# Attention scores of seven of eight pairs as three float32r products instead of one float32 product

## The chip, the cores and the metric

One core of a Trainium2 chip. The time is device microseconds of one execution, from the device's own measurement; the profile is of another execution of the same program. In the profile PE is TensorE (products), PEld its weight loads, DVE VectorE, ACT ScalarE, POOL GpSimd, SP SyncE, whose queue issues nearly all transfers. L56 is line 56 of the kernel before.

## The reference, cut to what matters

```python
scores = scale * np.matmul(q, k.transpose(0, 1, 3, 2))
h = np.maximum((psi_rel / psi_i)[..., None] @ w1 + b1, 0.0)
scores = scores + (h @ w2).transpose(2, 0, 1)[None, :, :, :]
attn = np.exp(scores - np.max(scores, axis=-1, keepdims=True))
attn = attn / (np.sum(attn, axis=-1, keepdims=True) + 1e-09)
x = np.matmul(attn, v)
```

q, k and v are float32 of 2 x 8 x 576 x 64 (batch, heads, sequence, head dimension). Two feed-forward networks follow on the 1152 rows of x: one with 2048 hidden columns and a rational activation, then four experts of 1024 with a gate. The change does not touch them.

## The kernel before, in words

The first 58 us make a position bias per head. Then comes the attention stage, to about 190 us, and the two networks fill the rest, TensorE nearly without a gap.

The attention stage works on eight **pairs** n = 0 to 7: two heads of one batch entry. The 64 dimensions of one head lie on partitions 0 to 63, those of the other on 64 to 127, so that each head's score product uses one half of TensorE's rows. A pair has nine **units** u. Unit u below eight is head u % 2 and block u // 2 of 128 of the 576 query rows; unit 8 is the last 64 rows of both heads, on the upper and the lower 64 output partitions. A call `scores(u)` for even u (lines 514 to 529) makes units u and u + 1: for each half of 288 key columns and each head one float32 product of 64 rows. VectorE then (line 527) adds the bias and takes the least, ScalarE's `exp` (line 536) makes the exponential and its sum, and VectorE's `weights` (line 543) transposes blocks of 32 for the product with v.

The order is written out by hand in one loop (lines 701 to 715), over the list of all units in order; only pair zero's last units stand among pair one's first. One step of the loop, called (n, u) here after its unit, issues: the scores of the unit two ahead, if that is even; what stands in the list `later`; `exp` of the next unit; `weights` of its own; and then `fill(n, u)` (lines 652 to 691). Every engine runs its instructions in the order in which they are issued. `fill` spreads the rest over the steps:

- values of the pair before, in (n, 1), (n, 3), (n, 5) and (n, 7) (line 576, into the tile ob); after the last of them three copies of o to SBUF on ScalarE (line 589), and, through `later` in (n, 8), `put` on GpSimd: one product with the reciprocal rows rs (line 594), two casts and two subtractions (lines 597 and 598).
- in (n, 5), for n from one to five, `prep(n + 2)`: ten transposes of raw q and k on TensorE into ob (line 181), and `load_qk` of the pair after that into the same raw tiles, six transfers. In (n, 6) four copies on ScalarE (`copied`, line 186) bring the transposed q (times 0.125) and k into the tiles qs and ks. Pair one is prepared in (0, 1), pair two in (1, 1).
- after (n, 8), `inverse`: reciprocal of the sums on VectorE and three copies on GpSimd (lines 551 and 554). In (n + 1, 6) `turn` transposes these on TensorE, and ScalarE copies them to rs (line 564).
- four early pieces of the first network's weights, one a pair from pair three on (lines 624 to 633, `EARLY` in line 697), through `later`: in (n, 4) ScalarE's narrowing (line 359), in (n, 5) to (n, 7) three steps on VectorE (lines 361, 363, 365), and in (n + 1, 0) the first part on ScalarE (line 369) and the second on GpSimd (line 375). They share one narrowed buffer: a piece's line 359 waits for the line 375 of the piece before.
- loads of v (line 163) in (n, 8), copies of v to the other partitions (line 167) in (n, 1), weight words in (2, 4), (3, 4), (5, 6) and (7, 3).

The score tiles of PSUM (tag s) have two buffers, which `turn` and the scores share.

## Time and profile before

| | us |
|---|---|
| median of 3 runs (779.59 to 781.68) | 781.19 |
| the profiled execution | 778.81 |
| its span in the trace | 777.0 |
| busy: PE, DVE, ACT, POOL | 758.7, 551.3, 428.9, 266.8 |

The span runs from the first to the last instruction; 1.8 us of the profiled execution lie outside of it. A busy time is a sum over the whole program, and PE's is 98% of the span, but it tells nothing of which engine is waited for within the attention stage. The granted clock of TensorE was at full speed throughout.

### The profile page before, as it was taken

Reading aid. Unit: us, or ns where it says so; the run is one execution under the profiler, and the core shown is the slowest. Engines: PE = TensorE matmul, PEld = TensorE weight load, DVE = VectorE, ACT = ScalarE, POOL = GpSimd, SP = SyncE. Lnnn points to the kernel's source line nnn. Section 1 sums busy time; section 2 is a strip of 40 time slices with the busy share of each in tenths; the row PEclk is TensorE's granted clock in tenths of the full one; section 3 lists DMA queues with packets and bytes.
Section 4 is the critical chain, followed back from the end, with each engine's and each line's share of the span. In section 5 each row is a group of like instructions: output and inputs, shape, how many; then the busy total and the mean of one; then the engine's idle time right before and its main releaser. Section 6 shows DMA issues by size and latency. Waiting matters only on the chain. (4 is left out here: it accounts for less than half of the span.)

```text
span 777.0 us, 15918 instructions
## 1 busy us (share of the span) xinstructions
PE 758.7 (98%) x6470; PEld 657.5 (85%) x6470; DVE 551.3 (71%) x873; ACT 428.9 (55%) x689; POOL 266.8 (34%) x278
## 2 busy tenths in 40 slices
PE   8998999999999999999999999999999999999998
PEld 5445766668899999999998989989989989988987
DVE  7998889996999999998954535567545645644731
ACT  6986667765988888787733525244314423413500
POOL 0000223442453655643300201236436534723710
PEclk9999999999999999999999999999999999999999
DMA  8899687551331331402123434332212202212201
GB/s 147 198 218 214 129 192 166 134 116 51 104 114 55 98 120 55 163 2 81 54 83 117 155 97 147 109 110 95 81 55 82 82 28 81 82 49 75 67 28 55
DMA packets 83946, 79.41 MB, mean 102 GB/s; under 512 B 38017, under 2 KB 62977, under 8 KB 83201
## 3 DMA queue, kind: packets, MB, share of 16 engines
q1 hardware_dynamic: 83440, 78.39, 37.3%
q8 instruction: 51, 0.84, 0.4%
q14 instruction: 23, 0.18, 0.1%
q10 hardware_dynamic: 432, 0.01, 0.0%
HBM read 59.20 MB, written 2.36 MB: 79 GB/s over the span
## 5 line engine op out<-in xcount | busy, mean ns | idle before, releaser
L56 PE MATMUL hp<-x,wi 128*128 128x384 f32 x888 | 159.7, 337 | 1.4 <-DVE u L776 1.1
L56 PEld LDWEIGHTS hp<-x,wi 128*128 128x128 f32 x888 | 154.0, 188 | 4.1 <-PE yp L56 1.5
L56 PE MATMUL op<-w,h 128*128 128x512 f32 (+1 forms) x600 | 133.1, 382 | 0.6 <-DVE acc L895 0.6
L56 PEld LDWEIGHTS op<-w,h 128*128 128x128 f32 x600 | 109.5, 188 | 22.4 <-DVE acc L895 0.8
L56 PE MATMUL yp<-g_hi,w 128*128 128x384 f32 x384 | 102.1, 336 | 0.3 <-ACT y L832 0.3
L895 DVE SCALAR_TENSOR_TENSOR acc<-op,pr_sb,acc 128x512 f32<-128x512 f32 (+1 forms) x28 | 20.4, 730 | 72.8 <-PE op L56 72.8
L56 PEld LDWEIGHTS yp<-g_hi,w 128*128 128x128 f32 x384 | 69.7, 188 | 1.2 <-ACT y L832 0.6
L536 ACT ACTIVATE pq<-pq,nm 128x576 f32<-128x576 f32 x72 | 55.4, 771 | 16.3 <-DVE nm L527 16.1
L56 PE MATMUL yp<-g_lo,w 128*128 128x384 f32 x192 | 64.2, 334 | 0.0
L373 POOL TENSOR_TENSOR w<-stage,w 128x256 fp32r<-128x256 f32 x64 | 49.1, 798 | 35.5 <-ACT w L369 35.5
L527 DVE CUSTOM_DVE_ANT_0 pq<-sc,ba 128x576 f32<-128x576 f32 x72 | 51.6, 749 | 13.3 <-PE sc L56 13.1
L417 ACT ACTIVATE wi<-stage 128x1024 fp32r<-128x1024 f32 x16 | 17.0, 1061 | 77.8 <-POOL stage L415 77.8
L56 PE MATMUL op<-w,h_hi 128*128 128x512 f32 x192 | 59.2, 389 | 0.0
L56 PE MATMUL sc<-ks,qs 64*128 64x288 f32 (+1 forms) x320 | 55.7, 429 | 2.7 <-DVE nm L527 1.9
L756 POOL TENSOR_TENSOR g_lo<-u,g_hi 128x768 fp32r<-128x768 f32 x24 | 45.1, 1880 | 35.8 <-ACT g_hi L755 33.8
L369 ACT ACTIVATE w<-stage 128x1024 fp32r<-128x1024 f32 x32 | 33.7, 1055 | 37.8 <-DMA stage<-in_moe_w_dram 37.7
L543 DVE STREAM_TRANSPOSE pt<-pq 128x576 f32<-128x576 f32 x72 | 52.1, 753 | 0.0
L576 PE MATMUL o<-pt,val 32*64 32x160 f32 (+1 forms) x2304 | 48.8, 293 | 2.3 <-issue 1.9
L232 PE MATMUL bps<-hid,wb 128*32 128x288 f32 x576 | 46.9, 410 | 3.2 <-DVE hid L221 2.3
L576 PEld LDWEIGHTS o<-pt,val 32*64 32x64 f32 x2304 | 39.2, 130 | 12.8 <-issue 5.9
L1038 ACT ACTIVATE h<-part_sums 128x384 fp32r<-128x384 f32 x48 | 25.1, 523 | 43.0 <-DVE part_sums L1058 34.4
L221 DVE TENSOR_SCALAR hid<-tab,cut 128x576 f32<-128x576 f32 x112 | 48.4, 522 | 0.0
(141 smaller groups left out, 1425.6 us busy)
## 6 DMA issues: line engine op xcount, KB each, us to landing
stage<-in_moe_w_dram SPq DMA_DIRECT2D x48, 512.0 KB, 3.6
ba<-ev SPq DMA_DIRECT2D x32, 288.0 KB, 5.4
words<-in_moe_w_in_dram SPq DMA_DIRECT2D x8, 1024.0 KB, 5.6
words<-in_moe_w_out_dram SPq DMA_DIRECT2D x8, 1024.0 KB, 5.0
stage<-in_moe_w_dram SPq DMA_DIRECT2D x64, 128.0 KB, 2.4
val<-val SPq DMA_DIRECT2D x21, 288.0 KB, 4.0
val<-in_v_dram SPq DMA_DIRECT2D x11, 288.0 KB, 4.1
out_dram<-acc SPq DMA_DIRECT2D x8, 256.0 KB, 2.0
```

The lines of the kernel that those rows point to most:

```text
L56: pe.matmul(o, lhsT=l, rhs=r, start=start, stop=stop)
L221: dve.tensor_scalar(tiles[par], win, at, 0.0, ALU.add, ALU.max)
L232: pe.matmul(sc[32 * par:32 * par + 32, hf, :288], lhsT=wb.rearrange("p r h -> p (r h)"), rhs=tiles[par][:, 288 * hf:288 * hf + 288], start ...
L369: act.activation(t[:, :, 0, :], self.raw, AF.Copy)
L373: pool.tensor_tensor(t[:, x[0], 1, x[1]], self.raw[:, x[0], x[1]], f32(t[:, x[0], 0, x[1]]), ALU.subtract)
L527: dve.tensor_tensor_reduce(out=self.row(u + e).rearrange("p (a j) -> p a j", a=2), in0=o[:, :, :288], in1=bs.rearrange("p (a j) -> p a j", ...
L536: act.activation(self.row(u), self.row(u), AF.Exp, bias=least.pop((self.n, u)), scale=-1.0, accum_out=self.sm[:, u:u + 1])
L543: dve.transpose(self.pt[:, 5 * e + k], self.row(u))
L576: pe.matmul(self.o[64 * e:64 * e + 64, a, c:c + 32 * m], lhsT=val[self.n % 2][r, NKB * e + b], rhs=self.pt[r, i:i + m, 32 * b:32 * b + 32] ...
L756: pool.tensor_tensor(lo, u, f32(hi), ALU.subtract)
L895: dve.scalar_tensor_tensor(out=a, in0=op, scalar=pr_sb[:, j, e:e + 1], in1=a, op0=ALU.mult, op1=ALU.add)
L1038: act.activation(t[:, 0], v, AF.Relu)
```

## The change

Pairs one to seven split q and k into a first part rounded to float32r and a second part, the rest, also in float32r. A score is then the sum of three products, accumulated in PSUM: first by first, first by second, second by first. Pair zero stays in float32. The four copies from ob now go back into the raw tiles; from there ScalarE makes the first parts and GpSimd subtracts to make the second, k in the next step through `later`, q in the step after that. The last 64 query rows of the two heads lie in a block matrix `both` of 128 x 128 with zeros off the blocks, so that unit 8 is three full products per half instead of two on quarters of the array. The raw tiles are free only after the split, so the load of k moves to (n, 8) and that of q to (n, 0). Two weight buffers change their pool to make room.

```diff
--- before.py
+++ after.py
@@ -147,10 +147,11 @@
 
     val = [rp.tile([P, 2 * NKB, D], F32, tag=f"v{i}", name="val") for i in range(2)]
 
-    def load_qk(n):
+    def load_qk(n, which=(0, 1)):
 
         p, b = divmod(n, 2)
-        for x, y in zip(raw(n), (q, k)):
+        for i in which:
+            x, y = raw(n)[i], (q, k)[i]
             h = y[b, 2 * p:2 * p + 2]
             for e in range(2):
                 sp.dma_start(x[:, 0:4, e], h[e, 0:512].rearrange("(t p) d -> p t d", p=P))
@@ -185,13 +186,11 @@
             w = 256 + 64 * a
             act.activation(x[:, 256 * a:256 * a + w], tp[:, a, 192:192 + w], AF.Copy, scale=scale)
 
-    def qs_tile(n):
-        q_of[n] = qk.tile([P, S], F32, tag="qs", name="qs")
-        return q_of[n]
-
-    def ks_tile(n):
-        k_of[n] = qk.tile([P, S], F32, tag="ks", name="ks")
-        return k_of[n]
+    def qk_tile(of, n, name):
+        of[n] = [qk.tile([P, S], F32R if n else F32, tag=name, name=name)]
+        if n:
+            of[n].append(lows.tile([P, 512 if name == "qs" else S], F32R, tag=name, name=name))
+        return of[n]
 
     def prep_first(x, to, scale):
         tp = ps.tile([P, 1024], F32, tag="s", name="tp_qk")
@@ -263,7 +262,7 @@
     load_qk(0)
     load_v(0, 4)
     BESIDE = {0: cut_near, 2: lambda: inverse_psi(psi), 5: cut_far}
-    BESIDE.update({6: lambda: prep_first(raw_q, qs_tile(0), 0.125), 7: lambda: (prep_first(raw_k, ks_tile(0), 1.0), load_qk(1), load_qk(2))})
+    BESIDE.update({6: lambda: prep_first(raw_q, qk_tile(q_of, 0, "qs")[0], 0.125), 7: lambda: (prep_first(raw_k, qk_tile(k_of, 0, "ks")[0], 1.0), load_qk(1), load_qk(2))})
     for r in range(4):
         dve.tensor_scalar(wb[:, r], w2c, pick[:, 3 - r:4 - r], None, ALU.mult)
     for m in range(AHEAD):
@@ -290,7 +289,7 @@
     pools = {}
 
     def wtile(tag, shape, dt, name, bufs=1):
-        return pools[tag in ("wi0", "words0", "words1", "narrow0")].tile(shape, dt, tag=tag, name=name, bufs=bufs)
+        return pools[tag in ("words0", "words1")].tile(shape, dt, tag=tag, name=name, bufs=bufs)
 
     class Weight:
 
@@ -352,7 +351,7 @@
             if not self.w.w64:
                 return
             if step == 0:
-                self.raw = wtile("narrow0" if self.early else f"narrow{turn('narrow', 2)}", self.shape, F32, "narrow")
+                self.raw = ap.tile(self.shape, F32, name="narrow", bufs=1) if self.early else wtile(f"narrow{turn('narrow', 2)}", self.shape, F32, "narrow")
             lo, hi = self.words[:, :, :, 0], self.words[:, :, :, 1]
             st, u = self.raw, self.raw.bitcast(U32)
             if step == 0:
@@ -477,6 +476,7 @@
 
 
     pools[True] = ctx.enter_context(tc.tile_pool(name="weights", bufs=2, reuse_waits="tile", side="right"))
+    lows = pool_of("lows")
     sp_, ap, pts = pool_of("scores"), pool_of("attn"), pool_of("pts", "right")
     po = phase.enter_context(tc.tile_pool(name="po", bufs=1, space=PSUM, reuse_waits="tile"))
 
@@ -488,6 +488,7 @@
         return x_t[cc][:, c]
 
 
+    both = [lows.tile([P, 2, P], F32R, name=f"both{i}", bufs=1) for i in range(2)]
     sums_z = ap.tile([P, P], F32, name="sums_z", bufs=1)
 
     ob = po.tile([P, 4, 512], F32, tag="o", name="o")
@@ -495,9 +496,28 @@
     def prep(n):
         for x, a in zip(raw(n), (0, 2)):
             turned(x, [ob[:, a + t // 2 - t // 4, 192 + P * (t % 2 + t // 4 * 2):min(512, 320 + P * (t % 2 + t // 4 * 2))] for t in range(5)], n < 3)
-        if 1 < n < NN - 1:
-            load_qk(n + 1)
-        soon.append(lambda: (copied(ks_tile(n), ob[:, 2:4], 1.0), copied(qs_tile(n), ob[:, 0:2], 0.125)))
+        if n == 2:
+            load_qk(3)
+        q32, k32 = (x.rearrange("p t e d -> p (t e d)")[:, :S] for x in raw(n))
+
+        def split(of, name, x):
+            t = qk_tile(of, n, name)
+            w = 512 if name == "qs" else S
+            hi, lo = t[0][:, :w], t[1]
+            act.activation(hi, x[:, :w], AF.Copy)
+            pool.tensor_tensor(lo, x[:, :w], f32(hi), ALU.subtract)
+            for e in range(2 * (name == "qs")):
+                r = slice(64 * e, 64 * e + 64)
+                hi, lo = (both[n % 2][r, part, r] for part in range(2))
+                act.activation(hi, x[r, w:S], AF.Copy)
+                pool.tensor_tensor(lo, x[r, w:S], f32(hi), ALU.subtract)
+
+        def whole():
+            copied(k32, ob[:, 2:4], 1.0)
+            copied(q32, ob[:, 0:2], 0.125)
+            later.append(lambda: (split(k_of, "ks", k32), later.append(lambda: split(q_of, "qs", q32))))
+
+        soon.append(whole)
 
     def keep_warm():
         for _ in range(4):
@@ -517,10 +537,15 @@
             self.pq[k] = sp_.tile([P, 2 * S], F32, tag="pq", name="pq", bufs=3)
             sc = [ps.tile([P, 2, 512], F32, tag="s", name="sc") for _ in range(2 - u // 8)]
             for hf in range(2):
-                for e in range(2):
-                    rows, cols = slice(64 * e, 64 * e + 64), slice(k * P, min(S, (k + 1) * P))
-                    out = sc[e][:, hf, :288] if u < 8 else sc[0][rows, hf, :288]
-                    mm(out, q_of[n][rows, cols], k_of[n][rows, 288 * hf:288 * hf + 288], True, True)
+                products = ((0, 0), (0, 1), (1, 0)) if n else ((0, 0),)
+                for i, (qpart, kpart) in enumerate(products):
+                    if n and u == 8:
+                        mm(sc[0][:, hf, :288], both[n % 2][:, qpart], k_of[n][kpart][:, 288 * hf:288 * hf + 288], i == 0, i == 2)
+                        continue
+                    for e in range(2):
+                        rows, cols = slice(64 * e, 64 * e + 64), slice(k * P, min(S, (k + 1) * P))
+                        out = sc[e][:, hf, :288] if u < 8 else sc[0][rows, hf, :288]
+                        mm(out, q_of[n][qpart][rows, cols], k_of[n][kpart][rows, 288 * hf:288 * hf + 288], i == 0, i + 1 == len(products))
             for e, o in enumerate(sc):
                 bs = bias[k, self.p // 2][:, self.p if u == 8 else 2 * (self.p % 2) + e]
                 nm = const.tile([P, 1], F32, tag="nm", name="nm", bufs=4)
@@ -672,6 +697,10 @@
             keep_warm()
         if u == 8 and 0 < n < NN - 1:
             load_v(n + 1)
+        if u == 8 and 0 < n < NN - 3:
+            load_qk(n + 3, (1,))
+        if u == 0 and 1 < n < NN - 2:
+            load_qk(n + 2, (0,))
         if (n, u) in COPY_V:
             copy_v(COPY_V[n, u])
         if u == (8 if n else 7):
@@ -703,8 +732,10 @@
             n, u = units[i + 2]
             if u % 2 == 0:
                 pair[n].scores(u)
-        if i == 2:
+        if i == 0:
             pool.memset(sums_z, 0.0)
+            for x in both:
+                pool.tensor_copy(x, sums_z.unsqueeze(1).to_broadcast([P, 2, P]))
         catch_up(later)
         if 0 <= i + 1 < len(units):
             n, u = units[i + 1]
```

## Rows read from the trace of the kernel before

**Rows 1.** Busy time in pair five: stretch, length; PE, PEld, DVE, ACT, POOL busy (count); clock; DMA.
```profile
134.06:149.13 15.07, 14.68 (x345) 10.22 (x344) 14.21 (x32) 11.01 (x30) 6.04 (x9) 1.00 0.60 151
```

**Rows 2.** Waits from 77 to 118 us: who waited for whom, us in all, times, longest.
```profile
DVE pq L527 <- PE sc L56: 6.0, 9, 1.2
```

**Rows 3.** Waits from 118 to 177 us, same columns.
```profile
ACT narrow L359 <- POOL w L375: 4.9, 3, 1.7
...
DVE pq L527 <- PE sc L56: 2.8, 7, 0.7
```

**Rows 4.** Timeline of ScalarE, rs of pairs four and six: start, us, what [idle before].
```profile
132.55 0.65 ACT L564 ACTIVATE rs<-rt 128x576 f32<-128x576 f32 x1 [1.10 <-PE rt L56]
...
161.75 0.65 ACT L564 ACTIVATE rs<-rt 128x576 f32<-128x576 f32 x1
```

**Rows 5.** Timeline of TensorE in pair five, and all scores: durations min/median/max.
```profile
139.11 1.24 PE L56 MATMUL sc<-ks,qs 64*128 64x288 f32 x8
...
140.28 1.64 PE L576 MATMUL o<-pt,val 32*64 32x160 f32 x80
...
L56 PEld LDWEIGHTS sc<-ks,qs x320: 129/186/243, 58.5 to 174.7; 64*128 64x128 f32 x128, 64*64 64x64 f32 x32
...
L56 PE MATMUL sc<-ks,qs x320: 402/403/507, 58.5 to 174.9; 64*128 64x288 f32 x128, 64*64 64x288 f32 x32
```

**Rows 6.** Timeline of TensorE, float32r products of 256 columns; the same by form: busy us, mean ns.
```profile
770.77 3.13 PE L56 MATMUL op<-w,h 128*128 128x256 f32 x24 [0.58 <-DVE acc L895]
...
L56 PE MATMUL op<-w,h 128*128 128x256 f32 x48 | 6.2, 285 | 0.6 <-DVE acc L895 0.6
```

**Rows 7.** Timeline of ScalarE in pair five.
```profile
136.27 0.93 ACT L589 ACTIVATE x<-o 128x512 f32<-128x512 f32 x3 [1.11 <-PE o L576]
...
138.00 0.61 ACT L369 ACTIVATE w<-narrow 128x512 fp32r<-128x512 f32 x1
...
143.71 0.68 ACT L359 ACTIVATE narrow<-words 128x512 f32<-128x512 f32 x1 [1.60 <-POOL w L375]
...
145.82 0.76 ACT L536 ACTIVATE pq<-pq,nm 128x576 f32<-128x576 f32 x1
...
147.62 0.65 ACT L564 ACTIVATE rs<-rt 128x576 f32<-128x576 f32 x1 [0.96 <-PE rt L56]
```

**Rows 8.** Timeline of GpSimd in pair five.
```profile
137.27 1.42 POOL L594 TENSOR_TENSOR x<-x,rs 128x576 f32<-128x576 f32 x1 [8.82 <-ACT x L589]
...
139.18 0.59 POOL L598 TENSOR_TENSOR x<-x,x 128x192 fp32r<-128x192 f32 x1
...
140.30 1.01 POOL L598 TENSOR_TENSOR x<-x,x 128x384 fp32r<-128x384 f32 x1
...
142.41 1.27 POOL L375 TENSOR_TENSOR w<-narrow,w 128x512 fp32r<-128x512 f32 x1
```

**Rows 9.** Loads of q, copies of o, transposes in pair two: SyncE, ScalarE, TensorE timelines; landing.
```profile
86.72 0.93 SPq L156 DMA_DIRECT2D raw_q<-in_q_dram  x2
...
DMA to landing us min/median/max: 2.4/3.4/7.5
...
90.58 0.93 ACT L589 ACTIVATE x<-o 128x512 f32<-128x512 f32 x3 [0.90 <-PE o L576]
...
97.25 0.86 PE L181 MATMUL o<-ident,raw_q 128*128 128x128 f32 x5
```

**Rows 10.** Timelines of ScalarE and TensorE around pair one's first scores.
```profile
65.53 0.70 ACT L186 ACTIVATE qs<-o 128x256 f32<-128x256 f32 x2
...
69.19 1.24 PE L56 MATMUL sc<-ks,qs 64*128 64x288 f32 x6 [0.46 <-DVE nm L527]
```

**Rows 11.** Line 363 and 365 in all: min/median/max ns; GpSimd beside the longest.
```profile
L363 DVE SCALAR_TENSOR_TENSOR narrow<-words,narrow x18: 685/1226/2761, 117.1 to 335.8; 128x1024 uint32<-128x1024 uint32 x14, 128x512 uint32<-128x512 uint32 x4
...
L365 DVE SCALAR_TENSOR_TENSOR narrow<-words,narrow x18: 686/1224/1268, 120.1 to 337.1; 128x1024 uint32<-128x1024 uint32 x14, 128x512 uint32<-128x512 uint32 x4
...
315.95 2.30 POOL L756 TENSOR_TENSOR g_lo<-u,g_hi 128x768 fp32r<-128x768 f32 x1
```

## The prediction

> **What bounds the kernel now.** The change lies in the attention stage, so I first split that stage by pair (the busy time of each engine in one pair's stretch, with its length). [Rows 1]: in pair five TensorE is busy for 14.68 of 15.07 us, VectorE for 14.21, ScalarE for 11.01, GpSimd for 6.04. Two engines are close together and the third not far; the totals do not say which one ends last, so I went to the waits. [Rows 2]: from 77 to 118 us VectorE waits nine times, 6.0 us in all, for scores from TensorE: there TensorE bounds. [Rows 3]: from 118 to 177 us it is only 2.8 us in seven waits, and ScalarE waits three times, 4.9 us, for GpSimd's second parts of an early weight before it may narrow the next piece into the same buffer (line 359 behind line 375). ScalarE works in order, so everything behind that wait is late too: three exponentials, then the reciprocal rows rs, then the two copies that empty the transposes. How much lateness is free there, the idle time just before rs shows: 1.10 us in pair four, 0.96 in pair five, none in pair six [rows 4, 7].
>
> **The products.** A call for an even u below eight is now eight records, 1.24 us from first start to last end; where nothing is waited for, the next group starts 1.17 us after it (139.11 to 140.28 [rows 5]). Eight records of 0.40 us and more fit into 1.24 us only if the two heads' run side by side, on the two halves of the rows: the last pair starts 0.84 us after the first, so a pair of records takes some 0.24 us, four of them 0.96, with 0.2 us around them. The new call has six pairs of single-pass products of 288 columns. float32r products on half the rows do not occur in this trace. On all rows they do: 24 of 256 columns take 3.13 us from first start to last end, and one record 0.285, so they start (3.13 - 0.285)/23 = 0.124 us apart [rows 6]; by columns that is 0.139 for 288. If the halves run together the call is 6 x 0.139 = 0.83 us, 0.13 less; 0.12 each (half of 0.24) would make it 0.24 less. If they don't, it is 12 x 0.139 = 1.67 us, 0.71 more. I take the first, since float32 on the same rows is nearest in form. For u = 8, of the same records now, it is six full products, 0.83, against four times 0.24: also 0.13 less. That is 0.65 us of TensorE per pair, 4.6 us over seven pairs, if every call were waited for.
>
> On that the Trainium skill (TensorE: Matmul & The Clock Gate, Part 3, What overlaps and what doesn't) speaks against the change: a weight load passes a running product only when their row groups differ. With its load of 128 columns at P/1.2 ns (LDWEIGHTS), 107 ns estimated, six steps would be 1.36 us (6 x (0.107 + 0.12)) instead of 0.83. The trace disagrees: each of the 256-column products above brought its own weights in the same rows, at 0.124 us a piece.
>
> **The splits.** ScalarE keeps its four copies, now into the raw tile, and per pair gets four more: k (576 columns), q (512, nearest row 0.61 us, line 369 [rows 7]) and two of 64 x 64. GpSimd gets the subtractions: 576 columns, 1.42 us as line 594; 512 columns, 1.27 us as line 375 in the same form; two of 64 columns. Line 598 took 0.59 for 192 and 1.01 for 384 [rows 8], that is 0.18 + 0.0022 per column, 0.32 for 64; between 0.18 and 0.59. In total 3.3 us of GpSimd and about 1.7 of ScalarE. By busy time both fit. What matters is the order. k's split goes out in the iteration of (n, 7), ahead of the copies of o, where GpSimd idles (8.82 us before line 594 [rows 8]): free. q's split goes out in (n, 8) **ahead of** the five operations of put, the three of inverse, and the early weight's line 375. So GpSimd's line 594, now starting as soon as the three copies of o end (137.20), first has to wait for ScalarE's first part of q (0.61), then 1.27 + 2 x 0.32: it starts 2.5 us later, and line 375 ends 2.5 us later. It starts as late as that in pairs four, five and six, where a next piece waits for it. ScalarE's line 359 then starts 2.5 us later, and so do the three exponentials behind it (the last at 145.82, 0.76 us [rows 7]) and rs. Free [rows 4, 7] are 1.10, 0.96 and 0: 3 x 2.5 - 2.06 = **5.4 us** later. After rs come TensorE's next scores (the second tile waits for rs), the copies of k and q, the values and the copies of o that begin the next round, so this lateness adds up over the three pairs, and in these rounds the shorter products save nothing. Bounds: 0 if GpSimd's work elsewhere gives way, and 7.5 if nothing is free.
>
> VectorE's transposes wait for the exponentials too. In (n, 8) the split of q is also ahead of the first exponentials of the next pair: 0.61 + 2 x 0.2 us. That is inside the 2.5 us in pairs four to six, and about 0.1 us in pairs two and three.
>
> **The loads.** k of pair n+3 moves to the end of pair n and q of pair n+2 to (n, 0); q now waits until the last subtraction has read the raw tile, and on SP the copies of val and the words of the early weights queue behind it, all used a pair later, at no cost. Pair two: the copies of o start at 90.58, 0.93 us; first part 0.61, subtractions 1.9, so the load is issued at about 94.1; two issues took 0.93 us, then the third lands 2.4 to 3.4 us (least and median) after its own, so q is there by 97.4 to 98.4. The transposes started at 97.25 [rows 9]. So pair two and three's transposes come 0.3 us later each (0 to 1.2) instead of 0.4 earlier by three shorter calls. In pairs four and five VectorE's own lateness covers it.
>
> **The start.** Pair one's copies end at 66.23 and its scores' last six records begin at 69.19 [rows 10]. In between now stand k's first part, an exponential, q's first part and 1.27 us of subtraction: 66.23 + 0.65 + 0.76 + 0.61 + 1.27 = 69.5. The third product waits 0.3 us for it (0 to 1).
>
> **Other edits.** The memset of sums_z and the two block tiles are filled while GpSimd has nothing to do before the first pair's weights; without that cover three copies of 0.3 us. One weight buffer and one narrowed buffer change pools; they are first written after the attention stage, whose tiles are free by then; without that, one wait of the first conversion, under 1 us.
>
> **Sum.** Gains: four calls from the middle of pair one to the first of pair two 0.52, the last call of pairs two and three and the first of the next 0.52, one in pair seven 0.13, together 1.2. Losses: 5.4 + 0.6 (loads) + 0.3 (start) + 0.1. Net +5.2 us. The profiled execution took 778.81 us (span 777.0), 2.4 us under the median of 781.19. So 778.8 becomes 784.0, and I say **786.4** for the median. A measurement of this kernel tells some 0.3%, 2.3 us, from no change.
>
> **Rivals.**
> 1. *The cover holds, faster.* If the early weight's subtraction is not late enough to matter (its wait is 1.6 us of 15 [rows 7], and GpSimd has 9 us free per pair [rows 1]), only products count: sixteen waits [rows 2, 3] of which each shrinks by 0.13 to 0.24, 2.1 to 3.8 us, less 0.3: 777.5 to 779.5. Against it: order, not load, decides. Chance 0.17.
> 2. *Between the two*: about half of the 5.4 us is lost. 779.5 to 783. Chance 0.09.
> 3. *The halves do not run together, much slower.* 28 calls of 0.71 more less 7 x 0.13 = +19 us, less what VectorE and the ScalarE chain need in the same time anyway: 793 to 800. For it: no float32r row on half the rows. Against it: float32 does it. Chance 0.13.
> 4. *Weight loads do not pass products of their own rows.* With the 0.19 us of a score's load [rows 5] in front of each step, six steps are 6 x (0.139 + 0.19) = 1.97 us, 1.0 more in 28 calls: 805 and over. Against it are [rows 6]. Chance 0.02. It is the rule of the Trainium skill weighed above.
> 5. *GpSimd gets in VectorE's way.* One operation of line 363 took 2.76 us where 1.23 is the median, beside a GpSimd subtraction that took 2.30 [rows 11]. k's subtraction will fall on line 365, of the same form, in pairs three to five: 3 x 1.5 = 4.6 us more if the later exponentials don't cover it, 787 to 791. Against it: eighteen of line 365 took at most 1.27 us [rows 11]. Chance 0.03. The Trainium skill (GPSIMD Engine Reference, Key points) has it that GpSimd shares its SBUF interfaces with VectorE, and that operations with two SBUF inputs collide; by that rule all three would pay, and the trace agrees in the one case only.
>
> The forecast, 783 to 790, has 0.58 (no wait free, 7.5 - 5.4 more, and the loads' 1.8 more, at its top; half of the 2.5 us less in one pair at its bottom), the five rivals 0.17, 0.09, 0.13, 0.02 and 0.03. The range 778.0 to 792.0 takes in all but the two much slower ones and the best of the first. Faster by over 0.3%: most of the first rival, 0.14. Within it: the rest of that and the second, 0.14. Slower: 0.72.
>
> **What would show it.** Right: records of 64-row products in pairs, six steps in about 0.8 us; ScalarE's three waits at line 359 near 4 us each; line 594 starting 2.5 us after the copies of o end; no idle before rs. Wrong: waits at line 359 as before, or score calls of 1.6 us and more.

## The result, and the profile after

The changed kernel takes **790.4 us** (median of 4 runs, 788.28 to 792.15), the kernel before 780.47 beside it (4 runs, 779.59 to 781.68): ratio 1.0125, 95% interval 1.0094 to 1.0156, 9.9 us slower. The forecast was 786.4, with a range from 778 to 792. The profiled execution took 789.86 us, its span 788.1, which is 11.1 more than before.

Where the 11.1 us arise is read from one operation that each call of the scores has once or twice, VectorE's step that adds the bias and takes the least for the exponential (line 527 before, line 552 now; I call it the exponent step). I took the start of the first one of a call (n,u) in the trace after, less its start before. The columns e1 and f1 belong to two experiments further down. "Before" is here one execution, of 778.81 us, 1.7 under the median beside the change: the columns tell where time is lost, and the medians how much.

| unit | before starts at | after, later by | e1, later by | f1, later by |
|---|---|---|---|---|
| (1,0) | 69.99 | 0.35 | 0.42 | 0.38 |
| (1,2) | 75.39 | 2.71 | 0.42 | 0.38 |
| (1,6) | 81.57 | 3.79 | 0.24 | 0.19 |
| (2,0) | 87.83 | 3.68 | 0.13 | 0.07 |
| (3,0) | 103.34 | 4.43 | 1.13 | 1.07 |
| (4,0) | 118.72 | 4.16 | 0.95 | 0.91 |
| (5,0) | 134.06 | 5.68 | 2.50 | 0.56 |
| (6,0) | 149.13 | 7.44 | 4.26 | 0.47 |
| (7,0) | 163.30 | 10.73 | 7.56 | 0.50 |
| (7,8) | 175.92 | 10.36 | 8.60 | -0.08 |

Three losses stand out: 2.4 us in one step from (1,0) to (1,2), another 1.1 by (1,6), and 6.6 from (4,0) to (7,0). Only the last of these was in the forecast.

**The products** became shorter. The timeline of TensorE after, three calls of pair one (start, length, what, count, idle before and who ended it):

```profile
74.46 1.11 PE L56 MATMUL sc<-ks,qs 64*128 64x288 f32 x12
76.75 0.66 PE L524 MATMUL o<-ident 128*128 128x128 f32 x4 [1.18 <-ACT raw L187]
78.88 0.40 PE L56 MATMUL sc<-ks,qs 64*128 64x288 f32 x1 [1.47 <-DVE nm L552]
79.56 1.34 PE L56 MATMUL sc<-ks,qs 64*128 64x288 f32 x11 [0.28 <-DVE nm L552]
80.84 3.51 PE L601 MATMUL o<-pt,val 32*64 32x160 f32 x112
84.27 1.06 PE L56 MATMUL sc<-ks,qs 64*128 64x288 f32 x12
```

and all records of the scores (nanoseconds, least, median and most):

```profile
L56 PEld LDWEIGHTS sc<-ks,qs x376: 129/184/335, 58.4 to 183.1; 64*128 64x128 f32 x184, 64*64 64x64 f32 x4
L56 PE MATMUL sc<-ks,qs x376: 285/292/605, 58.4 to 183.2; 64*128 64x288 f32 x184, 64*64 64x288 f32 x4
L56 PE MATMUL sc<-ks,both x42: 291/295/402, 88.1 to 185.3; 128*128 128x288 f32 x42
```

Twelve records now fit into 1.05 to 1.11 us where eight took 1.24 [rows 5]. In the call at 124.69 us two records, one on each half of the rows, start 3 or 4 ns apart, and from the second step on (124.92) the next two start 0.133 us later; only the first step takes 0.24. So the halves run together, and since a load of weights takes 0.18 us and each record has one of its own, the loads run beside the products. Where nothing is waited for, the next group starts 0.99 us after the first start (84.27 to 85.26), not 1.17.

**Pair one** has the two losses that were not foreseen. VectorE's timeline, the transposes of the exponentials, one row of before and then one of after:

```profile
74.04 1.43 DVE L543 STREAM_TRANSPOSE pt<-pq 128x576 f32<-128x576 f32 x2
```

```profile
76.73 1.44 DVE L568 STREAM_TRANSPOSE pt<-pq 128x576 f32<-128x576 f32 x2 [2.27 <-ACT raw L187]
```

and busy time in rows of 2 us, with TensorE's granted clock as the third number from the end (1.00 is the upper of its two levels, 2.4 GHz, and 0.50 the lower, 1.2 GHz; then the DMA engines' share and GB/s):

```profile
76.00:78.00 2.00, 0.66 (x4) 0.42 (x4) 1.26 (x2) 1.27 (x4) 0.59 (x1) 1.00 0.55 121
78.00:80.00 2.00, 0.83 (x7) 0.62 (x9) 2.00 (x6) 1.14 (x3) 0.81 (x1) 1.00 0.71 163
80.00:82.00 2.00, 2.00 (x46) 1.72 (x50) 2.00 (x5) 1.95 (x6) 1.60 (x3) 0.54 0.53 111
82.00:84.00 2.00, 2.00 (x85) 2.00 (x74) 1.80 (x6) 1.18 (x4) 1.28 (x4) 0.61 0.36 78
```

The transposes of the exps wait 2.27 us, which the profile puts down to ScalarE's copies of the next pair; TensorE then stands idle for 1.18 us (1.00 before) and 1.47 us with little between, and its granted clock is 0.50 from 80.2 to 83.5 us, so that 112 products with the values, 2.2 us before, take 3.5.

**Pairs four to six** look as forecast. Most lines have moved by the edit: 358, 364 and 374 are lines 359, 365 and 375 of the kernel before, 589, 614 and 619 are 564, 589 and 594. Waits from 122 to 186 us after (who for whom, us in all, times, longest):

```profile
ACT narrow L358 <- POOL w L374: 10.0, 3, 3.4
...
PE sc L56 <- ACT pq L561: 4.7, 3, 2.9
```

GpSimd's timeline in pair four:

```profile
123.76 1.41 POOL L508 TENSOR_TENSOR ks<-raw_k,ks 128x576 fp32r<-128x576 f32 x1 [5.17 <-ACT ks L507]
126.64 1.28 POOL L508 TENSOR_TENSOR qs<-raw_q,qs 128x512 fp32r<-128x512 f32 x1 [1.47 <-ACT qs L507]
127.88 0.70 POOL L513 TENSOR_TENSOR both<-raw_q,both 64x64 fp32r<-64x64 f32 x2
128.66 1.43 POOL L619 TENSOR_TENSOR x<-x,rs 128x576 f32<-128x576 f32 x1
...
133.79 1.27 POOL L374 TENSOR_TENSOR w<-narrow,w 128x512 fp32r<-128x512 f32 x1
```

and two rows of ScalarE's there, the copies of o and rs:

```profile
124.98 0.93 ACT L614 ACTIVATE x<-o 128x512 f32<-128x512 f32 x3 [0.60 <-PE o L601]
...
138.06 0.65 ACT L589 ACTIVATE rs<-rt 128x576 f32<-128x576 f32 x1
```

ScalarE's wait for the early weight's second part is 10.0 us where it was 4.9 [rows 3], the row of rs shows no idle before it, and TensorE waits for the first scores of the next pair, 4.7 us in three. From the first copy of o to the end of line 374 it is 10.1 us (124.98 to 135.06), before, in pair five, it was 7.4 (136.27 to 143.68 [rows 7, 8]).

One more row of pair four speaks for a rival. Line 364, the two-input step of VectorE that the prediction calls line 365, lies beside k's subtraction on GpSimd (123.76) and takes up to 1.48 us, against at most 1.27 before [rows 11]:

```profile
L364 DVE SCALAR_TENSOR_TENSOR narrow<-words,narrow x18: 686/1225/1480, 124.2 to 347.5; 128x1024 uint32<-128x1024 uint32 x14, 128x512 uint32<-128x512 uint32 x4
```

The pieces of 512 columns took 0.69 without a neighbour, so this one loses 0.79 us, and those of pairs five and six, at 1.43 and 1.42, some 0.74.

### The profile page after: what moved, and what is told of

Its sections match the earlier page's. It is cut to its first block, busy times and chain, and to the rows that moved or that the text cites. A ratio compares the mean times of both kernels' runs of the same rounds, so it can differ in the third digit from the quotient of the medians.

```text
span 788.1 us, 16187 instructions
## 1 busy us (share of the span) xinstructions
PE 755.0 (96%) x6568; PEld 666.2 (85%) x6568; DVE 553.4 (70%) x873; ACT 439.3 (56%) x717; POOL 290.4 (37%) x308
## 5 line engine op out<-in xcount | busy, mean ns | idle before, releaser
L601 PE MATMUL o<-pt,val 32*64 32x160 f32 (+1 forms) x2304 | 50.6, 302 | 7.9 <-ACT both L512 4.1
L56 PE MATMUL sc<-ks,qs 64*128 64x288 f32 (+1 forms) x376 | 43.4, 332 | 10.0 <-ACT pq L561 4.7
L601 PEld LDWEIGHTS o<-pt,val 32*64 32x64 f32 x2304 | 41.3, 136 | 13.9 <-issue 4.9
```

Source lines behind the costliest of these rows:

```text
L56: pe.matmul(o, lhsT=l, rhs=r, start=start, stop=stop)
L601: pe.matmul(self.o[64 * e:64 * e + 64, a, c:c + 32 * m], lhsT=val[self.n % 2][r, NKB * e + b], rhs=self.pt[r, i:i + m, 32 * b:32 * b + 32] ...
```

## Experiments

My theory after this reading: 3 us are lost to a buffer's place in pair one, 6 to 7 to GpSimd's queue in pairs four to six, and the longer line 364 is covered by the latter. The rivals: in pair one the transposes wait for ScalarE, as the profile says; line 364 is what holds the pairs; the loads or ScalarE's first parts do.

### 1. A buffer's place

The change takes two buffers out of the right-hand pool, and the pool of the transposed exps, which lies inward of it, moves outward. One of its two buffers would then overlap the last block of bias, whose last move into place lands at 76.66 us, just before the transposes begin. In the changed kernel (run e1):

```diff
-    lows = pool_of("lows")
+    lows = pool_of("lows", "right")
```

> The changed kernel with one edit: the pool of the second parts is opened on the right side, between the weights' pool and that of the transposed exps, so that the buffers of the transposed exps lie off the place where the last block of bias (t = 3) stands until its moves have landed. Theory (memory): pair one's first transposes, which began 2.27 us late at 76.7 us, waited for the last move of bias out of that block (landed 76.66). They then begin at about 74.5; the step (1,0) that was 0.35 us late stays so, (1,2) is 0.4 late instead of 2.7; TensorE's idle of about 1.5 us at 77.4 to 78.9 goes, and so its granted clock of 0.54 to 0.61 at 80 to 84 us, worth another 1.3. Sum -3.6: 786.8 us (785.8 to 788.0), where the changed kernel takes 790.4. Rival (engine): the transposes waited for ScalarE's copies of the next pair (ended 76.70), as the profile names them: the wait stays, 790.4 (789.5 to 791.5).

And in the kernel before the two buffers' move alone (run e4):

```diff
-        return pools[tag in ("wi0", "words0", "words1", "narrow0")].tile(shape, dt, tag=tag, name=name, bufs=bufs)
+        return pools[tag in ("words0", "words1")].tile(shape, dt, tag=tag, name=name, bufs=bufs)
...
-                self.raw = wtile("narrow0" if self.early else f"narrow{turn('narrow', 2)}", self.shape, F32, "narrow")
+                self.raw = ap.tile(self.shape, F32, name="narrow", bufs=1) if self.early else wtile(f"narrow{turn('narrow', 2)}", self.shape, F32, "narrow")
```

> The kernel before, with the change's move of two buffers alone: the first expert weight and the early float32 words leave the right-hand pool (which shrinks to 16 KB a partition), the words for the pool of the attention stage. No product, no split, no load is changed. Theory (memory): pair one's transposes wait for the last move of bias: about 2 us late there; with the drop of TensorE's clock behind it about 3.5 in all: 782.5 to 784.0 us against 780.5. Rival (engine, or the splits' copies): the move of buffers does nothing, 780.0 to 781.0.

Measured: e1 **787.28 us** (4 runs; before 780.14; ratio 1.0101, 1.0079 to 1.0123), 3.1 less than the change; e4 **782.42 us** (6 runs; ratio 1.0038, 1.0024 to 1.0052), 2.3 more than before: the theory's range, or within 0.1 us of it, both times. VectorE's timeline in e4, and the busy time there:

```profile
76.07 1.44 DVE L543 STREAM_TRANSPOSE pt<-pq 128x576 f32<-128x576 f32 x2 [1.98 <-DMA ba<-ev]
```

```profile
76.00:78.00 2.00, 0.66 (x4) 0.42 (x4) 1.93 (x3) 0.32 (x1) 0.00 (x0) 1.00 0.71 161
78.00:80.00 2.00, 1.78 (x6) 1.47 (x7) 2.00 (x6) 1.63 (x4) 0.00 (x0) 0.56 0.26 54
80.00:82.00 2.00, 2.00 (x36) 1.22 (x38) 1.65 (x6) 0.60 (x1) 0.00 (x0) 0.50 0.64 129
```

and the same stretch of VectorE in e1, with ScalarE's copies of the next pair:

```profile
74.46 1.44 DVE L568 STREAM_TRANSPOSE pt<-pq 128x576 f32<-128x576 f32 x2
```

```profile
75.49 1.28 ACT L187 ACTIVATE raw<-o 128x256 f32<-128x256 f32 x4
```

With the move alone, and ScalarE's copies where they were, the wait is there and now carries its real name, the move of bias; with the second parts' pool in between it is gone, though ScalarE's copies end no sooner (76.77), and so is the fall of the clock (1.00 from 76 to 84 us). The rival falls. In the trace after, ScalarE's copies had ended at 76.70 and the move landed at 76.66, and the profile took the later one. In the trace of e4 the wait and the clock behind it make 4.8 us by (1,6), of which 3.8 are left at the end of the span; the medians say 2.3, since the trace of before is of an execution 1.3 us under its median there.

### 2. The early weight's second part on VectorE

If line 374 is late on GpSimd, VectorE could do it. Run e2 changes one line of the changed kernel, e2b the same line of the kernel before, as a control:

```diff
-            self.w.eng.tensor_tensor(t[:, :, 1, :], self.raw, f32(t[:, :, 0, :]), ALU.subtract)
+            (dve if self.early else self.w.eng).tensor_tensor(t[:, :, 1, :], self.raw, f32(t[:, :, 0, :]), ALU.subtract)
```

> The changed kernel with one edit: the second part of the early weight (line 374) is made on VectorE instead of GpSimd, in pairs three to six. So the weight no longer stands behind q's split, the put, the inverse and the sums on GpSimd's queue, and line 358 on ScalarE has not to wait for it. Theory (chain): ScalarE's waits at line 358 (10.0 us in all, 3.3 at most) fall below 1 us each, and the rounds of pairs four, five and six, which took 16.9, 16.8 and 17.5 us, come to 15.2 to 15.8: the 1.5 + 1.8 + 2.5 that they lost, less about 0.3 each for the 0.6 to 0.7 us that VectorE works more, most of it in its idle time. Sum -4.9: 785.5 us (784.3 to 786.8). Rival: something else holds those pairs (the two-input step at line 364 that takes 1.45 us beside GpSimd, the copies of q ahead of the exps): less than 1.5 us is won, 789 to 790.5.

> The control of the run on the second part of the early weight: the same edit in the kernel before, where ScalarE waits 1.6 us and 3.3 us at that line (4.9 in all) but the row sums' factor still had about 1 us to spare. Theory (chain): this wait is paid only in part before, and VectorE's extra 0.6 to 0.7 us a pair eats what is won: 779.5 to 781.5 us, no difference to 780.5. Rival: the move to VectorE is good by itself, whatever the change does: 777 to 779.5.

Measured: e2 **792.37 us** (4 runs, ratio 1.0165, 1.0143 to 1.0188), slower than the change: a miss for the theory and for its rival. e2b 781.71 (9 runs, ratio 1.0020, 1.0003 to 1.0037), a little above its expectation (which has the three waits of 4.9 us before as two, of 1.6 and 3.3; they were 1.7, 1.6 and 1.6). VectorE and GpSimd in pair four of e2:

```profile
127.27 1.86 DVE L374 TENSOR_TENSOR w<-narrow,w 128x512 fp32r<-128x512 f32 x1
129.05 1.43 DVE L568 STREAM_TRANSPOSE pt<-pq 128x576 f32<-128x576 f32 x2
```

```profile
127.15 1.43 POOL L619 TENSOR_TENSOR x<-x,rs 128x576 f32<-128x576 f32 x1
```

ScalarE's wait at line 358 for the weight is gone, as expected. But the subtraction took 1.86 us on VectorE where 0.6 to 0.7 had been priced, beside GpSimd's line 619, which also reads two tiles. The transposes stand behind it, and TensorE behind them: it stood idle for 1.34 us before 131.2, and its granted clock was 0.52 from 132 to 134 and 0.62 to 136. So moving work from GpSimd to VectorE lost the time again twice, in a collision and in the clock. It says nothing against the chain, but it does not show it either.

### 3. GpSimd's subtractions left out, one at a time

Run e8 takes k's subtraction away (and with it the collision), e9 that of q (and with it the delay of GpSimd's queue), e5b both, all on top of e1. k's can go without moving q's, since q's waits for ScalarE anyway (1.47 us in the rows above).

```diff
-            pool.tensor_tensor(lo, x[:, :w], f32(hi), ALU.subtract)
+            if name == "qs":
+                pool.tensor_tensor(lo, x[:, :w], f32(hi), ALU.subtract)
...
-                        mm(out, q_of[n][qpart][rows, cols], k_of[n][kpart][rows, 288 * hf:288 * hf + 288], i == 0, i + 1 == len(products))
+                        mm(out, q_of[n][qpart][rows, cols], k_of[n][0][rows, 288 * hf:288 * hf + 288], i == 0, i + 1 == len(products))
```

(e8; in e9 the other name and the other factor, and the small blocks' subtraction too.)

> The changed kernel with the second parts' pool on the right side (787.3 us), and GpSimd's subtraction for k (line 508) left out: the products take k's first part in place of its second, as many of them and of the same shapes. q's split stands where it stood on GpSimd, since it waits for ScalarE's first part of q, not for k. Theory (collision): the two-input step of VectorE at line 364, 1.48 us beside this subtraction and 0.69 alone, stands on the path in pairs four, five and six, 0.75 us each, and falls to about 0.69: 785.0 us (784.2 to 785.9). Rival (chain alone): VectorE's longer step is covered by the later wait of the row sums' factor, the waits at line 358 stay: 787.3 (786.5 to 788.2).

> The changed kernel with the second parts' pool on the right side (787.3 us), and GpSimd's subtractions for q (lines 508 and 513 for q) left out: the products take q's first part in place of its second. k's subtraction, beside which VectorE's line 364 takes 1.48 us, stays. Theory (chain): GpSimd's put, inverse, sums and line 374 come 2 us or more sooner, ScalarE's waits at line 358 fall from 10.0 us to about 5, and the steps from (n,6) to the next pair's start lose the 1.0, 1.0 and 2.6 us that they are longer than before: 783.7 us (782.5 to 785.0). Rival (collision alone): the wait of ScalarE was not on the path; less than 1 us is won: 786.3 to 787.5.

> The changed kernel with the second parts' pool on the right side (787.3 us), and all of GpSimd's subtractions for q and k left out: the products take the first parts in place of the second, as many of them and of the same shapes; ScalarE's first parts stay. What is left of the change against the kernel before is the products, ScalarE's 12 more first parts and the loads. Theory (both causes on GpSimd, products a gain): 787.3 - 2.2 - 3.6 and nothing new: 781.3 or below, with the products' 0.13 to 0.2 us a call visible in TensorE's waits: 780.5 us (779.0 to 781.8). Rival (ScalarE's first parts or the loads hold it): 783 to 786.

Measured: e8 **788.79 us** (4 runs, 787.45 to 789.81), not under e1's 787.28 and above both expectations; e9 **781.30** (10 runs, 780.58 to 782.01), 1.2 under its theory's range; e5b **779.65** (10 runs, 779.24 to 780.45), within it; before 779.50 (25 runs). Waits from 118 to 190 us at line 358, in e1, e8 and e9, one row of each:

```profile
ACT narrow L358 <- POOL w L374: 10.1, 3, 3.4
```

```profile
ACT narrow L358 <- POOL w L374: 10.6, 3, 3.6
```

```profile
ACT narrow L358 <- POOL w L374: 1.1, 3, 0.8
```

and line 364 in e8 and e9:

```profile
L364 DVE SCALAR_TENSOR_TENSOR narrow<-words,narrow x18: 686/1224/1266, 123.9 to 346.3; 128x1024 uint32<-128x1024 uint32 x14, 128x512 uint32<-128x512 uint32 x4
```

```profile
L364 DVE SCALAR_TENSOR_TENSOR narrow<-words,narrow x18: 689/1225/1494, 120.6 to 338.6; 128x1024 uint32<-128x1024 uint32 x14, 128x512 uint32<-128x512 uint32 x4
```

In e8 the collision is gone and nothing is won: from (4,0) to (7,0) it loses 6.6 us against before, as e1 does. In e9 the collision stays, 1.49 us, and the chain is gone: from (4,0) to (7,0) it loses 2.2. So the chain sets these pairs, and the longer line 364 is covered by it; my expectation for e8 put it on the path and was wrong. It is not free, though: with the chain gone (e9) k's subtraction costs 1.65 us against e5b, and TensorE's idle ahead of the first products with the values is 1.4 us in pairs four to six of e9 and 0.64 in e5b. e5b cannot be told from the kernel before, so the third rival falls too: the loads and ScalarE's first parts hold nothing that the medians show.

### 4. The early steps in other places

If both are one matter of places, the early weight's steps can be moved so that VectorE's two-input steps come before k's subtraction, and GpSimd's line 374 between k's and q's. Run e6b, and f1 with the last piece ("half" in the expectations) left where it was; f3 is the kernel before with f1's move, as a control:

```diff
-    EARLY = [divmod(t + d, 9) for t in (30, 39, 48, 57) for d in (0, 1, 2, 3, 5)]
+    EARLY = [divmod(t + d, 9) for t in (30, 39, 48, 57) for d in (-1, 0, 1, 2, 3)]
```

```diff
+    EARLY = [divmod(t + d, 9) for t in (30, 39, 48, 57) for d in ((0, 1, 2, 3, 5) if t == 57 else (-1, 0, 1, 2, 3))]
```

> The changed kernel with the second parts' pool on the right side (787.3 us), and the early weights' five steps in another place: one unit sooner (four of them) and two units sooner (the split). VectorE's two-input steps then lie ahead of k's subtraction on GpSimd, and the weight's subtraction (line 374) comes on GpSimd between k's and q's, some 8 us sooner. Nothing is left out. Theory (both causes, collision and chain): line 364 takes 0.69 us again, line 358 waits for nothing from GpSimd; 2.2 + 3.6 us are won: 781.5 us (780.5 to 783.0). Rival: q's split, the put and the inverse stand 1.3 us later on GpSimd for it, ScalarE's split of the weight delays the exps, and other steps of VectorE meet GpSimd's two-input subtractions instead: 784.5 to 787.5.

> The changed kernel with the second parts' pool on the right side and the early weights' steps moved sooner for the first three halves alone; the last half keeps the units of the change. With all four halves moved 781.1 us were measured, 1.2 us of it lost between unit (6,6) and (7,0), where TensorE stood idle for 2.03 us behind VectorE, at the place of the last half's step at line 364, and its granted clock fell to 0.50 at 164 to 166 us. Pair seven has no split on GpSimd, so there is nothing there from which the last half would have to be moved away. Theory (the last half's step stands in the way): 780.0 us (779.0 to 780.8). Rival (the idle comes from pair six itself): 781.1 (780.6 to 782).

> The kernel before with the same move of the first three early halves' steps, as a control: is the move good by itself? Before, ScalarE waited 4.9 us in all at that line for GpSimd's weight, of which the row sums' factor covered about 1 us a pair. Theory (the move mends what the change had broken): little is won before, 779.0 to 780.3. Rival (the move is good for any kernel): 777.0 to 778.8.

Measured: e6b **781.12 us** (10 runs, ratio 1.0017, 1.0001 to 1.0033); f1 **778.93** (12 runs, 778.26 to 781.66; before 780.06 in 29 runs; ratio 0.9989, 0.9977 to 1.0001); f3 779.70 (12 runs, 0.9996, 0.9982 to 1.0011); the theory's range each time, f1 0.1 below it. GpSimd's timeline in f1:

```profile
120.52 1.43 POOL L508 TENSOR_TENSOR ks<-raw_k,ks 128x576 fp32r<-128x576 f32 x1 [5.26 <-ACT ks L507]
121.89 1.30 POOL L374 TENSOR_TENSOR w<-narrow,w 128x512 fp32r<-128x512 f32 x1
123.39 1.28 POOL L508 TENSOR_TENSOR qs<-raw_q,qs 128x512 fp32r<-128x512 f32 x1 [0.20 <-ACT qs L507]
124.63 0.71 POOL L513 TENSOR_TENSOR both<-raw_q,both 64x64 fp32r<-64x64 f32 x2
125.42 1.43 POOL L619 TENSOR_TENSOR x<-x,rs 128x576 f32<-128x576 f32 x1
```

and ScalarE's rs in the same pair, which has its idle time back:

```profile
132.94 0.65 ACT L589 ACTIVATE rs<-rt 128x576 f32<-128x576 f32 x1 [1.63 <-PE rt L56]
```

Line 374 now ends 3.6 us behind the pair's first exponent step (119.63 to 123.19), where it took 12.2 in the change (122.88 to 135.06); the wait at line 358 is absent from the list of f1, and line 364 takes at most 1.28 us over the program. The column f1 of the table shows that pairs four to six lose nothing any more; what stays is 1.0 us between (2,0) and (3,0). With nothing left out, f1 is 8.4 us faster than e1 and 11.5 faster than the change as made, more than the 9.9 that it had cost; f3 shows that the move is worth nothing that can be measured in the kernel before. f1 cannot be told from the kernel before, since the interval of the ratio reaches 1.0001.

### 5. What the products are worth

Run e10 puts the products alone into the kernel before: ScalarE's copies write float32r, and the three products take these; no split, no subtraction, no other load or buffer.

```diff
-        q_of[n] = qk.tile([P, S], F32, tag="qs", name="qs")
+        q_of[n] = qk.tile([P, S], F32R if n else F32, tag="qs", name="qs")
...
+                parts, v = (3, lambda x: x) if n and u < 8 else (1, f32 if n else lambda x: x)
...
-                    mm(out, q_of[n][rows, cols], k_of[n][rows, 288 * hf:288 * hf + 288], True, True)
+                        mm(out, v(q_of[n][rows, cols]), v(k_of[n][rows, 288 * hf:288 * hf + 288]), i == 0, i + 1 == parts)
```

(The same for ks. Where one product is made, v reads the tiles as float32.)

> The kernel before with the change's products alone: ScalarE's copies of q and k are written as float32r, and units zero to seven of pairs two to eight take three float32r products of these (first parts in place of the second) where one float32 product stood; the shared block keeps its float32 product, and there is no split, no subtraction, no second part, and the loads and buffers are those of before. Theory (the products are worth something in TensorE's waits): a call's two halves take 0.99 us instead of 1.17, and VectorE's waits for the scores shrink: 778.2 us (777.2 to 779.0). Rival (VectorE and ScalarE set the round): nothing, 779.2 to 780.5.

(Its pairs two to eight are pairs one to seven here.)

Measured: **778.89 us** (12 runs, 777.54 to 780.96; ratio 0.9986, 0.9972 to 1.0001). That is 1.2 us less, within the theory's range, and cannot quite be told from nothing. The trace does not show where it was won: the profiled execution has the span of before, 777.0 us, and its exponent steps are 1.1 to 2.0 us later than before from (2,6) to (7,4). The timeline of TensorE in pair two says where a part of it goes:

```profile
94.08 1.05 PE L56 MATMUL sc<-ks,qs 64*128 64x288 f32 x12
95.06 1.31 PE L578 MATMUL o<-pt,val 32*64 32x160 f32 x57
97.37 0.77 PE L578 MATMUL o<-pt,val 32*64 32x128 f32 x23 [1.00 <-issue]
98.07 1.06 PE L56 MATMUL sc<-ks,qs 64*128 64x288 f32 x12
```

The call is 0.18 us shorter, but among the products with the values TensorE stands idle for 1.00 us, and the profile names nothing that it waits for. Before, this group of 80 ran without a gap (94.31 to 95.87 us). f1 has the same idle of 0.79 at 96.75, and the changed kernel 0.53 at 100.1 and 1.09 at 188.2; the trace of the kernel before has such idle too in this stage, 0.60 us at most, and that of f3, which has its products, 1.57. What it is was not tried and stays open; the change has 418 records of the scores where there were 320, each with a load of weights.

## Why the prediction was right, and where it was not

The sum was +5.2 us and 9.9 were measured. The sign, the main mechanism and the range held, but 790.4 lies 0.4 us above the 783 to 790 of the forecast proper, and only because of a loss that the sum had at nothing; without it (e1, 787.3) it lies within. The fifth rival's 787 to 791 takes the time in too, but not for its reason, as is said below.

- **The products.** "I take the first": six steps of 0.139, 0.13 us less a call. Measured were steps of 0.133 and 0.18 less; the third and fourth rivals (halves apart, loads that don't pass) fall. The trace goes a second time against the rule of the Trainium skill weighed there (TensorE: Matmul & The Clock Gate, Part 3, What overlaps and what doesn't): each product brought weights into the rows on which the one before it was running, and the steps stayed at 0.133 us. The gain of 1.2 us is also e10's difference of medians, but its interval reaches zero and its trace shows no step sooner by as much: that the two agree shows nothing.
- **The splits.** Line 619 starts 2.8 us after the copies of o end (125.91 to 128.66), 2.5 were said; line 374 ends 2.7 later against its round; the waits at line 358 are 3.3 to 3.4 us each ("near 4"); no idle is left before rs. 5.4 us were forecast for pairs four to six. Measured from (4,0) to (7,0): 6.6, in the change and in e1 alike. The term is right in kind and 1.2 too small, and the clock is most of the difference: ahead of (7,0) TensorE waits 2.93 us, and eleven records of its call take 1.80 us where all twelve take 1.05 at the higher level:

```profile
171.78 0.37 PE L56 MATMUL sc<-ks,qs 64*128 64x288 f32 x1 [2.93 <-ACT pq L561]
172.41 1.80 PE L56 MATMUL sc<-ks,qs 64*128 64x288 f32 x11 [0.26 <-ACT rs L589]
```

```profile
172.00:174.00 2.00, 1.74 (x12) 1.46 (x11) 0.93 (x2) 1.11 (x3) 0.00 (x0) 0.58 0.03 8
```

In e1 another 1.0 us is lost behind (7,0), at a granted clock of 0.50 up to 175.5 us. e9 and f1 show the chain to be the cause: without it, whether by leaving q's subtraction out or by other places of the early steps, 6.0 and 8.4 us come back.
- **The start.** 0.3 forecast, 0.35 to 0.42 measured. e9, without q's subtraction, is 0.13 late there, and so is e5b: some 0.25 us are the wait that was forecast.
- **The loads.** 0.6 us forecast for pairs two and three; from (2,0) to (4,0) e1 loses 0.8. Right in size, but hardly for the reason: e10 has the loads of before and loses 1.3 there, with 1.5 us of unexplained idle on TensorE. Of the loads themselves a wait of 0.23 us is seen in pair four of e1 (TensorE for q at 129.6), and one of 0.93 in the change's pair five.
- **The exponentials behind q's first part.** 0.1 us forecast for pairs two and three, nothing for the others. In f1 each of pairs four to six loses 0.64 us from (n,2) to (n,4), ScalarE's first parts lying ahead of the exponentials there (e5b, with the first parts, loses 0.6 to 0.7 in the same places, e10, without them, 0.2 at most), and wins most of it back by (n+1,2): from (4,2) to (7,2) the sum is zero.
- **GpSimd in VectorE's way** (the fifth rival, 0.03). The collision happened in all three pairs, 0.73 to 0.79 us each rather than 1.5, and was covered by the later exponentials, as the rival allowed: e8 shows that nothing is won by removing it. The Trainium skill (GPSIMD Engine Reference, Key points) has it that GpSimd shares its SBUF interfaces with VectorE and contends with VectorE's operations of two SBUF inputs. The traces agree this time: 1.48 instead of 0.69 us at line 364, and 1.86 at line 374 in e2. I had weighed against it that line 365 never showed it before [rows 11]; but in those pairs GpSimd had been idle there (8.82 us ahead of its line 594 [rows 8], with line 365 at 135.42).
- **The step that failed** is "Other edits": one weight buffer and one narrowed buffer "are first written after the attention stage, whose tiles are free by then; without that, one wait of the first conversion, under 1 us". I asked only when the moved buffers themselves are written, and even that was wrong for the early pieces' narrowed one, which line 358 writes at 115.9 us, within the stage. Their pool shrank, and a third buffer that the diff doesn't name moved outward into the place of the last block of bias. That cost 2.3 us alone (e4) and 3.1 in the change (e1): a wait of 2.0 to 2.3 us and the fall of the clock behind it.

So of 9.9 us some 3 are of the buffer's place (3.1 by the medians of the change and e1, 2.8 when each is taken against the kernel before beside it) and 7.1 of the rest (e1 against its own 780.14), against 0 and 5.2 forecast.

## What to carry to other kernels

When an edit moves a buffer between pools, work out which other buffers change their place with it, and what those places still hold at that time; the diff does not name them. Before work is added to an engine's queue, find the operation on that queue for which another engine waits soonest, and put it first: here other places for five early steps, with the same work, were worth 8.4 us, and f1, with all subtractions, is no slower than e5b, with none. Giving work of one queue to another engine can cost more than it wins where the two collide (e2), so try another order first.

## What the runs showed of the hardware that was not expected

**A stall of TensorE can cost more than its wait, by the clock behind it.** Four stalls in this stage, as examples, that were followed by a stretch at the lower of the clock's two levels: in the change 1.47 us of idle (0.50 from 80.2 to 83.5 us) and 2.93 us (0.50 from 172.4 to 175.6), in e4 1.00 and 1.19 us with little between (0.50 from 78.3 to 85.0), in e2 1.34 us (0.52 and 0.62 in the next two rows of 2 us). What the lower clock cost on top of the wait is 1.1 us in pair one of the change and 2.7 in e4, by the exponent steps from (1,2) to (1,6), and 0.75 us in the call of (7,0); in e2 it cannot be parted from the collision. None of it was in the sum. Not every such stall brought it: 1.35 us of idle in the change's pair four (138.13) and 1.45 in f1's pair six (162.72) were followed by 1.00.

It can also fall where nothing in the program differs. In pair zero, whose products are the same in all these kernels, the profiled execution of e8 shows

```profile
60.00:62.00 2.00, 1.50 (x8) 0.67 (x7) 1.44 (x4) 0.90 (x3) 0.00 (x0) 0.98 0.92 220
62.00:64.00 2.00, 2.00 (x7) 0.96 (x8) 0.77 (x2) 0.82 (x3) 0.00 (x0) 0.50 0.98 189
64.00:66.00 2.00, 2.00 (x10) 1.54 (x9) 1.95 (x4) 1.64 (x4) 0.40 (x2) 0.50 0.93 252
```

where that of the kernel before has

```profile
60.00:62.00 2.00, 1.50 (x8) 0.67 (x7) 1.44 (x4) 0.89 (x3) 0.00 (x0) 1.00 1.01 213
62.00:64.00 2.00, 2.00 (x13) 1.27 (x12) 1.39 (x5) 1.32 (x3) 0.00 (x0) 1.00 0.98 199
```

after the same 1.50 of 2.00 us of work. That execution is 2.8 us later than e1's at (1,0), and that of e2b 3.1 later than the kernel before. In f3 it followed the 1.57 us of idle for which the profile names nothing, in pair three:

```profile
110.81 1.03 PE L56 MATMUL sc<-ks,qs 64*128 64x288 f32 x5 [1.57 <-issue]
111.77 2.97 PE L576 MATMUL o<-pt,val 32*64 32x160 f32 x80
```

The 80 products take 1.64 us in the kernel before [rows 5], and that execution is 3.0 us later by (3,6) than at (3,2). Such falls are a part of the scatter among runs of the kernel before: of the 29 beside f1, the 22 with a mean granted clock of 0.999 or more took 779.4 us on average and the other seven 781.5. They are likely a part of e8's 1.5 us over e1 as well; this is why e8 is judged by its steps from (4,0) to (7,0) above.
